# A gated attention with channel mix on one core: all engines in one written order, one scan over four pairs, the second square on ACT, weights in contiguous pieces

## Chip, cores and metric

The kernel runs on one core of one Trainium2 chip. The metric is the device time of one execution in microseconds. The kernel before took 393.07 us, the median of three runs (390.4 to 397.02).

## The reference

Two layers in float32: a linear attention with a decaying state for 4 batches, 8 heads, 768 steps, head size 48, and a channel mix of 384 features with 1024 inner ones.

```python
for t in range(S):
    state = alpha[:, :, t, :, None] * state + einsum('bhd,bhe->bhde', k[:, :, t], v[:, :, t])
    y[:, :, t] = einsum('bhd,bhde->bhe', q[:, :, t], state)
...
xk = mu_k * x + (1 - mu_k) * x_prev        # x: y with the heads side by side
xr = mu_r * x + (1 - mu_r) * x_prev        # x_prev: the row of the step before
k = maximum(xk @ w_k, 0)
v = k * k @ w_v
r = 1 / (1 + exp(-(xr @ w_r)))
out = r * v
```

## The kernel before

**Tiles.** The 24 chunks of 128 steps lie in nine groups, each within one batch: groups 0 to 2 have two chunks (256 columns), groups 3 to 8 have three (384). Heads lie in four pairs, two heads of a pair on partitions 0 to 47 and 64 to 111.

**Attention of a group.** `load` fetches alpha (`al`), k, q and v. `prep_p` makes the running product of alpha, one forward scan per pair (L258), the reciprocal of its last column (L262), and on ACT a check that no alpha is over 1 (`junk`, L265). `prep_gh` multiplies q by the product (L276), scans backward from that reciprocal, again one scan per pair (L281), and multiplies k by it (L284); tables give each product to DVE or POOL, most queries to DVE, most keys of groups of three chunks to POOL. A chunk then needs: `trans`, transposes of k through TensorE (L336) and ACT's copy `ht` (L338); `scores` (L346) and the mask on DVE (`am`, L352); `update` (L399) and `advance`, the state sums on DVE (L411, L415, L417); `intra` and `inter` (L365, L383); `leave` (L425, L431). One `visit` handles `intra`, `inter` and `leave` of a chunk together with `update`, `scores` and `advance` of the next. After the last chunk two DMAs copy borrowed rows inside `xt` (L438), from SP for group 0 and from ACT for the others.

**Channel mix of a group.** `mix` forms xk and xr (i = 0 and 1): for each of three feature tiles a scaling on ACT (L478), a sum on DVE (L479), a rounded high part on ACT (L482) and the difference as low part on DVE (L483). `moe` lists the pieces of TensorE's work: 8 up slices of 9 matmuls (L500), a gate of 9 per chunk (L525), a down of 24 per chunk (L540). Each product of float32 numbers is three products of high and low parts. After an up slice ACT takes the positive part `r` (L508); r squared in float32 comes from ACT in groups 0 and 1 (L510) and from DVE in the others (L512); ACT squares r once more into the rounded high part `kh` (L513), and DVE subtracts to get `kl` (L514). After a down, DVE multiplies by the gate (L545), and SP stores.

**Weights** come as raw words. `split` makes high and low parts of a piece: ACT copies the top half words (L208), DVE shifts and joins (L213), ACT or DVE rounds the high part (L219, L221), POOL or DVE subtracts (L222). There are four pieces of the up, two of the gate and four of the down weights.

**Order.** TensorE and SP follow the written order; ACT, DVE and POOL are ordered by the planner of the framework. `merge` lays the attention of group g+1, with weights, among the pieces of the channel mix of group g; then comes `mix` of g+1. From group 1 on, the load and the whole of `prep` for group g+2 stand at the start of that attention. For group 0 a table `FILL` says at which step weight pieces and the preparations of groups 1 and 2 are put in.

Of the kernel before, what the change touches and what calls it, by code (L numbers as in the profile page):

```python
# [42 lines left out]
LEAD = 12.0  # L43
LEAD0 = 8.0
PAD = 3.0
ENG = {
    "wk": ("AP", "AD", "AP", "AP"),
    "wr": ("DP", "DP"),
    "wv": ("DP", "DP", "AD", "DP"),
}  # L50
K2 = "AAD"
QH = ("DDDD", "PDPD", "PPPP")
QG = ("PDDD", "DPDP", "DDDP")
FILL = [
# [3 lines left out]
]  # L58
FIRST_LOADS = ["k", "wk0", "al", "wk1", "q", "wk2", "wk3", "v"]
WARM = 22  # L60
HOLD = 14
NX = HB - D
# [4 lines left out]


def merge(main, side, lead):
    total = max(sum(w for w, _ in main) - lead, 1.0)  # L70
    load = sum(w for w, _ in side)
    done = spent = 0.0
    side = list(side)
    for w, f in main:
        f()
        done += w
        while side and spent / load <= done / total:
            ws, fs = side.pop(0)
            fs()
            spent += ws  # L80
    for _, fs in side:
        fs()
# [3 lines left out]
def gated_attention_channel_mix(  # L86
# [17 lines left out]
    PE, ACT, DVE, POOL = nc.tensor, nc.scalar, nc.vector, nc.gpsimd  # L104

# [8 lines left out]
    zero = cp.tile([R, R], F32, name="zero")  # L114
    POOL.memset(zero, 0.0)

    hot = pm.tile([R, R], F32, tag="pm", name="hot")
    with tc.manual_schedule(engines={mybir.EngineType.PE}):
        for i in range(WARM):
            PE.matmul(hot, zero, zero, start=True, stop=True)  # L120

    none, *rings = (cp.tile([R, NP * D + HB - D], F32, name=f"st{i}") for i in range(5))
    for t in (none, *rings):
        POOL.memset(t, 0.0)
    tiny = cp.tile([128, 1], F32, name="tiny")
    POOL.memset(tiny, FLOOR)
    mone = cp.tile([128, 1], F32, name="mone")
    POOL.memset(mone, -1.0)
    ones = cp.tile([128, 1], F32, name="ones")
    POOL.memset(ones, 1.0)  # L130
    ACT.activation(ones, ones, AF.Sigmoid)
    POOL.memset(ones, 1.0)
    racc = cp.tile([128, 2 * NG], F32, name="racc")
# [3 lines left out]
    mu = cp.tile([128, 2, NT], F32, name="mu")  # L137

    loaded = {}

    def span(g):
# [678 lines left out]
```

## Time and profile before

| | |
|---|---|
| median of three runs | 393.07 us |
| the profiled execution | 391.8 us |
| its span, first to last instruction | 390.1 us |
| TensorE matmul busy | 332.0 us (85%) |
| DVE busy | 281.6 us (72%) |
| ACT busy | 188.7 us (48%) |
| POOL busy | 65.3 us (17%) |
| mean granted TensorE clock | 0.923 |
| DMA | 35.56 MB, mean 91 GB/s |

An instruction is named by its line, engine, operation and tiles (out<-in). A row of groups gives the count, busy time, mean duration in ns, and the idle time of that engine just before, with what ended it. A row of the timeline gives start and length in us. Ends of matmuls are modelled, and matmuls overlap. POOL's spans are rough.

### The profile page before, as it was taken

How to read it: one execution, taken by the hardware profiler on the slowest of the kernel's cores; microseconds unless marked ns; L12 is line 12 of the kernel's file. 1: busy time of each engine (PE TensorE's matmuls, PEld its weight loads, DVE VectorE, ACT ScalarE, POOL GpSimd, SP SyncE). 2: the span in 40 equal slices, each digit the busy share in tenths (PEclk: the TensorE clock that was granted, in tenths of full speed). 3: DMA queues.
4: the chain of work that ended last, by engine and by line, in shares of the span. 5: the costliest groups of instructions: out<-in, count | busy, mean ns of one | idle time of the engine just before them, and what ended most of it. 6: DMA issues, size and time to landing. Idle time of an engine off the chain costs nothing.

```text
span 390.1 us, 10751 instructions
## 1 busy us (share of the span) xinstructions
PE 332.0 (85%) x4590; PEld 315.5 (81%) x4590; DVE 281.6 (72%) x513; ACT 188.7 (48%) x393; POOL 65.3 (17%) x84
## 2 busy tenths in 40 slices
PE   7542787709995997899979997999999999999993
PEld 6432687709984996799969997999999999999993
DVE  5787989998389639988596959678965476456510
ACT  3356693236563345544355525562754555455500
POOL 5143544550021003203010220003000000000000
PEclk9655769968999799999999998999999999999998
DMA  8978455830703070305510341025100110011001
GB/s 212 273 249 293 136 152 143 233 91 24 212 25 92 12 214 22 91 3 172 142 42 2 100 144 42 3 74 169 44 2 2 37 43 3 3 37 40 0 23 47
DMA packets 15958, 35.56 MB, mean 91 GB/s; under 512 B 1600, under 2 KB 9568, under 8 KB 15904
## 3 DMA queue, kind: packets, MB, share of 16 engines
q1 hardware_dynamic: 14736, 33.72, 29.2%
q10 hardware_dynamic: 1168, 1.09, 1.1%
q8 instruction: 38, 0.62, 0.7%
q14 instruction: 16, 0.13, 0.1%
HBM read 28.90 MB, written 4.72 MB: 86 GB/s over the span
## 4 chain that ended last, share of the span: by engine, by line
PE 47%; DVE 20%; DMA 6%; issue 4%; ACT 3%; ACTq 0%; DVEq 0%
PE pk L500 19%; PE pv L540 13%; PE pg L525 5%; DVE al L281 4%; DMA xt<-xt 4%; DVE pp L258 4%; DVE x L479 3%; PE yu L365 2%; DMA q<-q_p 2%; DVE xkl L483 2%; DVE q L276 1%; PE pt L336 1%; DVE kl L514 1%; PE sp L346 1%; PE yu L399 1%
## 5 line engine op out<-in xcount | busy, mean ns | idle before, releaser
L500 PE MATMUL pk<-xkh,wkh 128*128 128x384 f32 (+1 forms) x216 | 51.4, 345 | 21.7 <-ACT xkh L482 21.7
L540 PE MATMUL pv<-wvh,kl 128*128 128x384 f32 x192 | 64.9, 338 | 2.4 <-DVE kl L514 2.4
L540 PE MATMUL pv<-wvl,kh 128*128 128x384 f32 x192 | 64.7, 337 | 0.0
L540 PE MATMUL pv<-wvh,kh 128*128 128x384 f32 x192 | 64.4, 335 | 0.0
L500 PEld LDWEIGHTS pk<-xkh,wkh 128*128 128x128 f32 x216 | 37.9, 203 | 24.5 <-ACT xkh L482 23.6
L508 ACT ACTIVATE r<-pk 128x384 f32<-128x384 f32 (+1 forms) x72 | 32.3, 454 | 41.2 <-PE pk L500 38.4
L500 PE MATMUL pk<-xkh,wkl 128*128 128x384 f32 (+1 forms) x216 | 49.6, 340 | 0.0
L500 PE MATMUL pk<-xkl,wkh 128*128 128x384 f32 (+1 forms) x216 | 48.6, 335 | 0.1
L284 POOL TENSOR_TENSOR k<-k,al 112x768 f32<-112x768 f32 (+1 forms) x18 | 31.1, 1733 | 91.3 <-DVE al L281 50.0
L512 DVE TENSOR_TENSOR k<-r 128x384 f32<-128x384 f32 (+1 forms) x56 | 30.0, 535 | 22.7 <-ACT r L508 22.1
L478 ACT ACTIVATE x<-xt,mu 128x384 f32<-128x384 f32 (+1 forms) x54 | 28.5, 575 | 35.6 <-DMA xt<-xt 25.5
L514 DVE TENSOR_TENSOR kl<-k,kh 128x384 fp32r<-128x384 f32 (+1 forms) x72 | 36.7, 509 | 11.0 <-ACT kh L513 5.8
L281 DVE TENSOR_TENSOR_SCAN al<-al 112x383 f32<-112x383 f32 (+1 forms) x36 | 39.7, 1137 | 1.3 <-ACT junk L265 1.1
L500 PEld LDWEIGHTS pk<-xkl,wkh 128*128 128x128 f32 x216 | 38.4, 203 | 0.8 <-DVE xkl L483 0.3
L540 PEld LDWEIGHTS pv<-wvh,kl 128*128 128x128 f32 x192 | 36.1, 188 | 3.4 <-DVE kl L514 3.4
L500 PEld LDWEIGHTS pk<-xkh,wkl 128*128 128x128 f32 x216 | 37.2, 202 | 0.9
L258 DVE TENSOR_TENSOR_SCAN pp<-al,tiny 112x384 f32<-112x384 f32 (+1 forms) x36 | 33.9, 963 | 4.2 <-DMA al<-al_p 4.2
L540 PEld LDWEIGHTS pv<-wvl,kh 128*128 128x128 f32 x192 | 36.0, 188 | 0.0
L540 PEld LDWEIGHTS pv<-wvh,kh 128*128 128x128 f32 x192 | 36.0, 188 | 0.0
L513 ACT ACTIVATE kh<-r 128x384 fp32r<-128x384 f32 (+1 forms) x72 | 34.7, 488 | 1.4
L479 DVE SCALAR_TENSOR_TENSOR x<-xt,nu,x 128x384 f32<-128x384 f32 (+1 forms) x54 | 31.9, 631 | 2.7 <-ACT x L478 2.7
L425 ACT COPY xt<-yu 112x512 f32<-112x512 f32 x24 | 14.1, 588 | 35.8 <-DVE st L415 25.3
(149 smaller groups left out, 531.3 us busy)
## 6 DMA issues: line engine op xcount, KB each, us to landing
out<-sig SPq DMA_DIRECT2D x24, 192.0 KB, 1.9
al<-al_p SPq DMA_DIRECT2D x6, 672.0 KB, 5.3
k<-k_p SPq DMA_DIRECT2D x6, 672.0 KB, 4.7
q<-q_p SPq DMA_DIRECT2D x6, 672.0 KB, 7.4
v<-v_p SPq DMA_DIRECT2D x6, 600.0 KB, 4.2
wkraw<-wk_p SPq DMA_DIRECT2D x4, 768.0 KB, 14.6
vraw<-wv_p SPq DMA_DIRECT2D x4, 768.0 KB, 5.5
v<-v_p SPq DMA_DIRECT2D x3, 400.0 KB, 6.6
```

Source lines behind the costliest of these rows:

```text
L258: DVE.tensor_tensor_scan(pp[:, p], al[:, p, :n], tiny[:R].to_broadcast([R, n]), initial=START, op0=ALU.mult, op1=ALU.max,)
L281: DVE.tensor_tensor_scan(back, back, back, initial=al[:, i, n : n + 1], op0=ALU.mult, op1=ALU.bypass)
L284: (DVE if QH[min(g, 2)][p] == "D" else POOL).tensor_tensor(k[:, hp], k[:, hp], al[:, hp, 1:], op=ALU.mult)
L478: ACT.activation(x, xt[:, t, 1 : 1 + n], AF.Copy, scale=mu[:, i, t : t + 1])
L479: DVE.scalar_tensor_tensor(x, xt[:, t, 0:n], nu[:, i, t : t + 1], x, op0=ALU.mult, op1=ALU.add)
L500: PE.matmul(pk, w[:, t, cols], x[:, t], start=part == 0 and t == 0, stop=part == 2 and t == NT - 1,)
L508: ACT.activation(r, pk, AF.Relu)
L512: DVE.tensor_tensor(k2, r, r, op=ALU.mult)
L513: ACT.activation(kh[:, f], r, AF.Square)
L514: DVE.tensor_tensor(kl[:, f], k2, kh[:, f].bitcast(F32), op=ALU.subtract)
L525: PE.matmul(pg, x[:, i, cols], w[:, i], start=part == 0 and i == 0, stop=part == 2 and i == NT - 1,)
L540: PE.matmul(pv, x[:, f, cols], w[:, f], start=f == 0 and i == 0, stop=f == NF - 1 and i == 2,)
```

## The change

All five engines now follow one written order. `prep_p` and `prep_gh` become `fwd`, `bwd`, `qm` and `km`: one forward and one backward scan per group run over all four pairs at once. Each pair gets one more column, in which alpha is 0, and the second operand `fl` of the scans holds a start value in that column (2^30 forward, the reciprocal of the product's last column backward), so that the scan starts anew; elsewhere `fl` holds the floor 2^-50. All q products go to POOL, one chunk and then the rest; of the k products chunk 0 goes to DVE, the rest to POOL.

```diff
-        for p in range(p0, p0 + m):
-            DVE.tensor_tensor_scan(
-                pp[:, p], al[:, p, :n], tiny[:R].to_broadcast([R, n]), initial=START,
-                op0=ALU.mult, op1=ALU.max,
-            )
...
+    def fwd(g):
...
+        DVE.tensor_tensor_scan(
+            flat(pp), flat(al), fl[:, : NP * (n + 1)], initial=START, op0=ALU.mult, op1=ALU.max
+        )
+        junk = p1.tile([R, NP, n + 1], U8, tag="r", name="junk")
+        ACT.activation(junk, al, AF.Relu, bias=mone[:R], accum_out=racc[:R, g : g + 1])
+        DVE.reciprocal(breaks(n), pp[:, :, n - 1])
...
+    def bwd(g):
+        n = span(g)[3]
+        back = flat(loaded["al", g])[:, ::-1]
+        DVE.tensor_tensor_scan(
+            back, back, fl[:, : NP * (n + 1)][:, ::-1], initial=0.0, op0=ALU.mult, op1=ALU.max
+        )
+        if g + 1 < NG:
+            if span(g + 1)[3] != n:
+                POOL.memset(breaks(n), FLOOR)
+            POOL.memset(breaks(span(g + 1)[3]), START)
```

`mix` is called once for each half, with one buffer `x` for three tiles, and makes the three low parts in one instruction. After an up slice ACT squares once in float32; the rounded high part is a copy, on DVE in groups 0 and 1 and on ACT in the others. It comes a little later in the order.

```diff
-            r = p2.tile([128, n], F32, tag="r", name="r")
-            k2 = p1.tile([128, n], F32, tag="k2", name="k2")
+            r = p1.tile([128, n], F32, tag="r", name="r")
             ACT.activation(r, pk, AF.Relu)
-            if K2[min(g, 2) if type(g) is int else 2] == "A":
-                ACT.activation(k2, r, AF.Square)
-            else:
-                DVE.tensor_tensor(k2, r, r, op=ALU.mult)
-            ACT.activation(kh[:, f], r, AF.Square)
-            DVE.tensor_tensor(kl[:, f], k2, kh[:, f].bitcast(F32), op=ALU.subtract)
+            sq = p2.tile([128, n], F32, tag="sq", name="sq")
+            ACT.activation(sq, r, AF.Square)
+            later(0.6, lambda: low(f, sq))
...
+        x = p1.tile([128, NT, n], F32, tag="x", name="x")
         for t in range(NT):
-                x = p2.tile([128, n], F32, tag="x", name="x")
+            ACT.activation(x[:, t], xt[:, t, 1 : 1 + n], AF.Copy, scale=mu[:, i, t : t + 1])
...
+        for t in range(NT):
+            ACT.activation(hi[:, t], x[:, t], AF.Copy)
+        DVE.tensor_tensor(lo, x, hi.bitcast(F32), op=ALU.subtract)
```

In group 0 the downs of both chunks go slice by slice (`across`). The host lays each weight piece out so that a partition reads it in one run; loads are whole tensors; the loads of group 0, of the up weights, of group 1 and of the gate weights are issued in this order, then the down weights. The raw up weights lie in the buffers of the later down weights. The borrowed rows of group 0 are copied from ACT's queue as well. The warm-up of TensorE grows from 22 to 30 products.

The order is a list of marks: a mark is put in before the first piece of TensorE's channel mix whose place (sum of the weights of the pieces before it, near microseconds) is not smaller. `trans` of a chunk is now 0.4 before the first visit and 1.6 before the others.

```diff
+SIDE = {
+    1: (0.2, 5.6, 9.2, 12.2, 15.4),
+    2: (0.2, 5.2, 8.2, 11.2, 13.6, 16.4),
+    3: (0.2, 5.6, 8.8, 12.4, 15.8, 18.4),
+}
+KH = "DDAAAAAAA"
...
+            if g == 0:
+                marks += [
+                    (1.2, lambda: fwd(1)),
+                    (2.5, lambda: qm(1, 0, 1, "P")),
+                    (4.0, lambda: bwd(1)),
...
+                    (6.3, lambda: (begin(1), mix_group(0, 1))),
+                    (7.4, lambda: (trans((1, 0)), visit(None, (1, 0)))),
+                    (7.5, lambda: (conv("r", 0, "A"), conv("r", 1, "A"))),
...
+                    (8.2, lambda: visit((1, 0), (1, 1))),
+                    (8.25, lambda: conv("v", 0, "A")),
+                    (8.3, lambda: (load_al(2), visit((1, 1), None))),
+                    (8.5, lambda: conv("v", 1, "A")),
...
+                    (10.5, lambda: conv("v", 2, "A")),
+                    (11.5, lambda: conv("v", 3, "A")),
+                    (12.5, lambda: (mix_in(1, span(1)[3]), mix_group(1, 0))),
+                    (14.5, lambda: mix_group(1, 1)),
+                    (17.0, lambda: fwd(2)),
...
+                def start_h(h=h, m=m):
+                    bwd(h)
+                    km(h, 0, 1, "D")
+                    km(h, 1, m - 1, "P")
...
+                def after(h=h):
+                    if h + 1 < NG:
+                        fwd(h + 1)
+                        qm(h + 1, 0, 1, "P")
+                        qm(h + 1, 1, GROUPS[h + 1][2] - 1, "P")
+
+                marks.append((at[0], start_h))
+                marks.append((at[0] + 0.1, loads))
+                marks.append((at[1] - 0.4, lambda u=units[0]: trans(u)))
+                marks.append((at[1], lambda u=units[0]: visit(None, u)))
...
+                t0 = at[2 + m]
+                marks.append((t0, mixes))
+                marks.append((t0 + 2.0, lambda h=h: mix_group(h, 1)))
+                marks.append((t0 + 4.5, after))
```

Before these marks, group 0 is prepared as a whole, its attention runs with the first two pieces of the up weights among it, then its first mixed half and the other two pieces (`conv`: `split_top`, `split_or`, `split_hi`, `split_lo`). Group 1 as main group takes row 1 of `SIDE`, group 2 takes row 2, the others take row 3.

More of the change, by code (lines that the diff above doesn't have):

```diff
@@ L42 @@
 DW = D // DQ
[L43 to L49, printed above, removed]
-}
[L51 to L54, printed above, removed]
[3 rows of a table removed]
[L58 to L62, printed above, removed]
+WP = 2 * DM
+WARM = 30
+NX = HB - D
+UP, GATE = 0.16, 0.52
+SIDE = {
+    1: (0.2, 5.6, 9.2, 12.2, 15.4),
+    2: (0.2, 5.2, 8.2, 11.2, 13.6, 16.4),
+    3: (0.2, 5.6, 8.8, 12.4, 15.8, 18.4),
+}
+KH = "DDAAAAAAA"
 def head(i, o):
     return 2 * (2 * (i >> 1) + o) + (i & 1)
[L69 to L82, printed above, removed]
 @with_exitstack
@@ L112, in gated_attention_channel_mix @@
     dp = ctx.enter_context(tc.tile_pool(name="dp", bufs=1, space=DRAM))
[L114 to L120, printed above, removed]
     none, *rings = (cp.tile([R, NP * D + HB - D], F32, name=f"st{i}") for i in range(5))
[L123 to L126, printed above, removed]
+    fl = cp.tile([R, NP * (GMAX + 1)], F32, name="fl")
     mone = cp.tile([128, 1], F32, name="mone")
-    POOL.memset(mone, -1.0)
     ones = cp.tile([128, 1], F32, name="ones")
[L130 to L133, printed above, removed]
+    racc = cp.tile([128, NG], F32, name="racc")
     pbeg = cp.tile([128, NG * NP], F32, name="pbeg")
@@ L192, in gated_attention_channel_mix, with load_al @@
[L192 to L206 removed]
+    def load_al(g):
+        b, c0, nck, n = span(g)
+        t = p2.tile([R, NP, n + 1], F32, tag="al", name=f"al{g}")
+        loaded["al", g] = t
+        at = NP * (b * S + c0 * C + g)
+        nc.sync.dma_start(
+            t.rearrange("r p t -> r (p t)"), al_p[:, at : at + NP * (n + 1)]
+        )
@@ new lines, in flush, with spend, run @@
+    def flush(all_=False):
+        while True:
+            ready = [d for d in due if all_ or d[0] <= clock[0] + 1e-9]
+            if not ready:
+                return
+            d = min(ready)
+            due.remove(d)
+            d[2]()
+    def spend(w):
+        clock[0] += w
+        flush()
+    def run(pieces, marks):
+        marks = sorted(marks, key=lambda m: m[0])
+        t = 0.0
+        for w, f in pieces:
+            while marks and marks[0][0] <= t + 1e-9:
+                marks.pop(0)[1]()
+            f()
+            t += w
+            spend(w)
+        for _, f in marks:
+            f()
@@ new lines, in scores @@
+    def scores(u, sp):
+        g, c = u
+        h, q = loaded["k", g], loaded["q", g]
+        for p in range(NP):
+            for s, j in sides:
+                rr = slice(j * HB, j * HB + D)
+                t0 = c * C + s * HC
+                PE.matmul(
+                    sp[s * HC : (s + 1) * HC, j, p * HC : (p + 1) * HC],
+                    h[rr, p, t0 : t0 + HC], q[rr, p, t0 : t0 + HC],
+                    start=True, stop=True,
+                )
+        am[u] = p2.tile([C, 2, NP, HC], F32, tag="am", name=f"am{g}_{c}")
+        DVE.tensor_tensor(
+            am[u], sp[:, :, : NP * HC].rearrange("c j (p t) -> c j p t", p=NP),
+            mask.unsqueeze(1).unsqueeze(1).to_broadcast([C, 2, NP, HC]), op=ALU.mult,
+        )
```

751 lines of the change are left out of this document (376 added, 375 removed), and 3 rows, old and new, of the table FILL.

## The prediction

> **What bounds the kernel now.** I read the work of each engine in ten windows first, cut where a group's first up matmul starts. Columns: length, busy microseconds of PE, weight loads, DVE, ACT and POOL with counts, granted clock, DMA.
>
> ```profile
> 0.00:35.00 35.00, 17.04 (x308) 15.09 (x308) 24.82 (x42) 14.27 (x22) 15.30 (x36) 0.68 0.86 247
> 35.00:84.70 49.70, 32.40 (x402) 30.19 (x402) 47.99 (x73) 26.34 (x62) 24.24 (x20) 0.81 0.55 163
> 84.70:114.90 30.20, 27.84 (x386) 26.49 (x387) 20.73 (x45) 19.30 (x51) 1.34 (x4) 0.90 0.33 99
> 114.90:154.40 39.50, 32.35 (x536) 30.20 (x536) 29.79 (x58) 16.86 (x40) 7.05 (x7) 0.91 0.32 89
> 154.40:195.20 40.80, 38.43 (x552) 36.43 (x551) 34.12 (x59) 19.95 (x41) 7.19 (x6) 1.00 0.35 98
> 195.20:236.20 41.00, 38.40 (x570) 36.64 (x569) 32.35 (x60) 20.79 (x43) 5.43 (x6) 1.00 0.24 68
> 236.20:278.00 41.80, 39.60 (x553) 37.91 (x552) 34.22 (x65) 22.02 (x45) 4.54 (x5) 0.96 0.23 72
> 278.00:315.80 37.80, 37.80 (x568) 36.41 (x567) 24.43 (x51) 20.43 (x40) 0.19 (x1) 1.00 0.06 21
> 315.80:353.80 38.00, 38.00 (x554) 36.61 (x553) 21.96 (x46) 19.10 (x37) 0.00 (x0) 1.00 0.07 22
> 353.80:390.10 36.30, 30.10 (x174) 29.49 (x172) 11.23 (x22) 9.62 (x19) 0.00 (x0) 0.97 0.07 24
> ```
>
> Groups 6 and 7 are PE alone: 37.9 us each, PE never idle. Group 8 has no attention beside it: 30.1 us of PE, so a chunk of attention costs PE (37.9-30.1)/3 = 2.6. Before 84.7 the limit is DVE, busy 48.0 of 49.7 us in group 0. Then the waits of PE, and its timeline, which show where those windows are cut:
>
> ```profile
> PE pk L500 <- ACT xkh L482: 21.7, 6, 9.3
> PE pt L336 <- DVE k L284: 6.7, 5, 2.6
> PE yu L365 <- DVE am L352: 4.6, 3, 2.4
> ...
> 22.20 0.92 PE L346 MATMUL sp<-q,k 48*64 48x64 f32 x23 [1.47 <-issue]
> 25.03 1.14 PE L365 MATMUL yu<-am,v 64*64 64x64 f32 x32 [1.91 <-DVE am L352]
> 35.02 0.98 PE L500 MATMUL pk<-xkh,wkh 128*128 128x256 f32 x2 [8.00 <-ACT xkh L482]
> ...
> 84.70 0.97 PE L500 MATMUL pk<-xkh,wkh 128*128 128x256 f32 x2 [9.28 <-ACT xkh L482]
> 87.88 0.58 PE L500 MATMUL pk<-xkh,wkh 128*128 128x256 f32 x1 [2.20 <-ACT xkh L482]
> ...
> 353.77 0.68 PE L500 MATMUL pk<-xkh,wkh 128*128 128x384 f32 x3
> 354.29 0.68 PE L500 MATMUL pk<-xkh,wkl 128*128 128x384 f32 x3
> ```
>
> Here is to be seen that PE waits for two things: for the first mixed half of a group (xkh: 8.0, 9.3 and 2.2 us, the work that DVE was late with), and for keys and masked scores. At full clock three matmuls of 384 columns take 0.52 us, nine (one up slice) 1.56.
>
> **Working of the change.** The sum is made against this execution: span 390.1, its time 391.8, so 1.7 us lie around the span; it is 1.3 under the median of 393.07.
>
> *Until the first up matmul (35.0 now).*
>
> ```profile
> 4.19 1.27 DVE L258 TENSOR_TENSOR_SCAN pp<-al,tiny 112x256 f32<-112x256 f32 x2 [4.19 <-DMA al<-al_p]
> 12.50 0.42 DVE L284 TENSOR_TENSOR k<-k,al 112x256 f32<-112x256 f32 x1
> 17.65 4.09 DVE L258 TENSOR_TENSOR_SCAN pp<-al,tiny 112x256 f32<-112x256 f32 x4
> ```
>
> The keys of group 0 are ready at 12.9. With whole loads alpha lands later (twice the bytes of the first piece, an estimate of 5.1), then two scans of 2.4 each, a reciprocal 0.2, 0.8 lost to POOL and a key product 0.7 (prices below) give 11.6: minus 1.3. The scan of group 1 (4.09) no longer stands in front of the masks, so the waits of 1.5 and 1.9 go: minus 3.4. The last hop of 8.0 becomes 5.2 from the last visit to the landed rows less its own 1.0, 2.5 for the half and 0.8 for queueing, 7.5: minus 0.5. Sum 29.8; bounds 27 (every wait gone) and 35. Weights in pieces three times as long cost nothing: the windows show 247 GB/s before 35.0 and no PE wait on a weight load; their cover is the DVE chain. The last-column zeros of al_p and the longer warm-up lie in the first 12 us.
>
> *Group 0 (49.7 now).* What DVE has to do before the first mixed half of group 1 is there, at these prices:
>
> ```profile
> L213 DVE SCALAR_TENSOR_TENSOR rraw<-rraw,tops 128x768 uint32<-128x768 uint32 x1 | 1.0, 962 | 0.5 <-ACT tops L208 0.5
> L514 DVE TENSOR_TENSOR kl<-k,kh 128x256 fp32r<-128x256 f32 x24 | 10.0, 416 | 5.4 <-ACT kh L513 3.8 <-ACT k L510 1.2
> L352 DVE TENSOR_TENSOR am<-sp,mask 128x512 f32<-128x512 f32 x15 | 10.2, 683 | 1.6 <-PE sp L346 1.6
> L222 POOL TENSOR_TENSOR wvl<-vraw,wvh 128x768 fp32r<-128x768 f32 x3 | 6.1, 2039 | 8.7 <-DVE wvh L221 8.7
> L276 POOL TENSOR_TENSOR q<-q,pp 112x256 f32<-112x256 f32 x4 | 4.4, 1117 | 4.5 <-PE sp L383 3.8 <-DMA q<-q_p 0.6
> L258 DVE TENSOR_TENSOR_SCAN pp<-al,tiny x36: 659/943/2326, 4.2 to 241.4; 112x384 f32<-112x384 f32 x24, 112x256 f32<-112x256 f32 x12
> L281 DVE TENSOR_TENSOR_SCAN al<-al x36: 717/1005/2237, 5.8 to 264.3; 112x383 f32<-112x383 f32 x24, 112x255 f32<-112x255 f32 x12
> ```
>
> A scan of 256 columns takes 0.66, one of 384 takes 0.94: 2.2 ns a column and 0.1 fixed. So one scan over four pairs is 2.4 us for 1028 columns, 3.5 (backward 3.6) for 1540: it saves three fixed parts, some 0.3, and holds DVE in one piece. Restart columns: no row; their bounds are 0 and the four columns' 9 ns. DVE list: shift-or of seven pieces at 0.96 and a half one, 7.3; two casts, 1.1; eight casts of kh moved from ACT, no row of that form, between 0.1 and 0.42, taken 0.3: 2.4; eight kl at 0.42, 3.3; two scans 4.8; a key product 0.7; two mixed halves (three sums at 0.42 and one merged difference at 0.96 each), 4.4; two masks at 0.68 and nine state and output sums of 128 to 192 columns, each under the 0.42 of 256 and taken at 0.31, 4.2. Together 28.2. POOL meanwhile: seven low parts of 2.04, one of 1.0, three products of 512 columns at 1.6 (between 1.12 and 2.04): 20.1. POOL and DVE hinder each other:
>
> ```profile
> 178.43 1.01 DVE L281 TENSOR_TENSOR_SCAN al<-al 112x383 f32<-112x383 f32 x1 [0.35 <-ACT junk L265]
> 179.81 4.07 DVE L281 TENSOR_TENSOR_SCAN al<-al 112x383 f32<-112x383 f32 x3
> 180.96 2.11 POOL L284 TENSOR_TENSOR k<-k,al 112x768 f32<-112x768 f32 x1 [13.60 <-DVE al L281]
> ```
>
> Three scans take 4.07 instead of 3.03 while a POOL product of 2.11 runs: 0.5 us of DVE for each of POOL, so 10.0. With 2.3 for ACT, which stands between its two halves of each weight piece until DVE has done the shift-or, group 0 takes 40.5; bounds 32 (28.2 and a third of the rest) and 50 (as now). The Trainium skill, SBUF — State Buffer, section Who interferes with whom, says more: a DVE instruction with two SBUF inputs and a reading GpSimd one exclude each other, and the later waits the whole length. By that page alone the 10.0 would be 20.1, and the sum 394; the row shows half of it. It speaks against this change, which hands POOL all query products and two thirds of the keys.
>
> *The chain from group to group.* Now the products for a group are ready a group ahead. In the written order forward scan and backward scan of the next group stand behind both mixed halves of this one:
>
> ```profile
> 339.04 0.69 PE L365 MATMUL yu<-am,v 64*64 64x64 f32 x32
> 340.97 1.22 ACTq L438 DMA_DIRECT2D xt<-xt  x2
> 344.21 1.12 ACT L478 ACTIVATE x<-xt,mu 128x384 f32<-128x384 f32 x2 [1.43 <-DMA xt<-xt]
> L513 ACT ACTIVATE kh<-r 128x384 fp32r<-128x384 f32 x48 | 25.2, 526 | 1.1
> ```
>
> From the last visit to the landed rows 5.2 us; each half 4.5 (three scalings at 0.56, the last sum at 0.6, the last rounding 0.53, then one difference of 1152 columns, 1.4; the second half waits for it, x having one buffer), 9.0; an output product 0.5; forward scan 3.5, reciprocal 0.2, backward scan 3.6, key product 0.7. Sum 22.7 until the next group's transposition can start. PE's list prices its pieces in microseconds (nine up matmuls 1.56, three others 0.52): 29.6 for a group of 384 columns, 19.7 for one of 256. The last visit stands at 15.8, the next group's transposition at 5.2, so PE is there after 13.8, 1.1 for the visit and 5.2: 20.1. So PE stands 2.6 there: groups 4 to 7 take 37.9+2.6 = 40.5, together 162.0. Group 2 has 256 columns and its last visit at 13.6: 6.1+1.1 are left, the first mixed half comes at 8.3, so 1.1 of wait, and the chain ends 9.2 behind PE in group 3: 47.1. In group 1 the halves cost 3.4 (256 columns), the chain 20.5, PE is there after 7.5+1.1+4.8 = 13.4 (last visit at 12.2): 7.1 in group 2, whose own work is 28.5 (group 1's 27.0 from 87.9 to 114.9, less about 1.1 of cold start, plus a chunk of 2.6): 36.7. In group 1 the second half, both scans and the key stand 9.4 behind the first one, PE is there after 5.2: 4.2, with 25.9 of its own 30.1. Group 8 keeps 36.3.
>
> The queues that are passed: SP's loads go out ahead of the outputs but into buffers that came free a group earlier; the two DMAs of borrowed rows move to ACT for group 0 (0.6 each there, under the flight between the last two dated rows). The third ACT instruction per up slice makes three of at most 0.53, 1.6 us against 1.56 of PE, and its cover is the 2.6 us of attention per chunk; without it 0.04 a slice. The square that leaves DVE from group 2 on (one pass a slice) frees DVE in windows where PE does not wait for it, so by itself nothing.
>
> **Sum.** 29.8+40.5+30.1+36.7+47.1+162.0+36.3 = 382.5, with 1.7 outside 384.2, called 384. The beginning gives 14; the chain gives 7 of it back.
>
> **Rivals.** *Covered chain:* if halves and scans overlap more than the order says, or PE has other work ahead of the transposition, the four terms 4.2, 8.2, 9.2 and 10.4 go: 352; half of them 368. For it: groups 6 and 7 show PE can run at 37.9. Against: one x buffer and DVE in written order. *Slower by the shared way of POOL and DVE:* the query products (1.6 and about 2.5) start with the forward scan's end, just as the backward scan and the key product do. If POOL goes first each time, 4.1 us more per group, in groups 1 to 7: 28.7, giving 413; it is slower by 2% once it costs 2.4 a group. For it: the 4.07 row; against: that row shows half the length. The Trainium skill's page SBUF — State Buffer stands on this rival's side. *No gain in the beginning:* ACT waits inside each weight piece and group 1 starts at 84.7 as now: 14.4 more, 398. *It doesn't do what it says:* the order now is already near the written one and nothing moves: 392.
>
> **How the numbers follow.** Forecast 0.44 (its own range 372 to 397: 0.25 faster, 0.17 same, 0.02 slower), covered 0.24 (0.23 faster), POOL 0.12 (0.10 slower, 0.02 same), beginning 0.12 (0.01, 0.09, 0.02), nothing 0.08 (0.01, 0.06, 0.01). Faster 0.50, same 0.35, slower 0.15, where 2% is about what a measurement of this kernel can tell from no change. Range 356 to 404: the half-covered chain below, all but the full POOL price above; outside it some 0.09 and 0.11.
>
> **What would show it.** First up matmul near 30 and group 1's near 70; then PE waiting, in front of the first transposition of each group, for the key product of chunk 0, longest in group 3 (about 9 us), 2 to 3 us in groups 4 to 7, none in group 8; forward scans of 3.5 and backward ones of 3.6 us. Wrong if groups 3 to 7 take 38 us each, if a scan takes over 5, or if group 1 starts after 80.

## The result, and the profile after

The changed kernel takes 447.03 us (median of 4 runs, 446.22 to 448.51), the kernel before 391.74 beside it: a ratio of 1.143, 95% interval 1.137 to 1.149. The forecast was 384. Ratios here compare undisturbed runs, and one run of a later kernel, with 415.89 us at a granted clock of 0.804, is left out of its figures. The profiled execution took 448.51 with a span of 446.7. Its windows, cut at each group's first up matmul, with the columns of the prediction's first fence:

```profile
0.00:35.98 35.98, 17.58 (x324) 16.14 (x325) 17.46 (x28) 9.44 (x16) 14.36 (x24) 0.66 0.86 289
35.98:91.62 55.64, 37.09 (x403) 34.06 (x403) 36.88 (x51) 28.03 (x52) 19.97 (x16) 0.70 0.17 50
91.62:125.57 33.95, 29.10 (x387) 27.64 (x387) 22.19 (x41) 15.15 (x37) 6.79 (x8) 0.90 0.35 101
125.57:165.68 40.11, 31.05 (x535) 29.14 (x534) 24.73 (x37) 18.75 (x45) 10.62 (x8) 0.87 0.28 82
165.68:218.99 53.31, 42.22 (x551) 39.15 (x552) 32.55 (x43) 28.76 (x57) 10.62 (x7) 0.90 0.20 58
218.99:265.94 46.95, 41.73 (x569) 39.50 (x568) 27.91 (x40) 23.65 (x47) 10.84 (x8) 0.93 0.27 75
265.94:313.61 47.67, 41.98 (x553) 39.52 (x552) 26.93 (x38) 23.64 (x47) 10.63 (x7) 0.93 0.25 73
313.61:361.05 47.44, 41.74 (x567) 39.57 (x568) 28.13 (x40) 23.64 (x47) 10.83 (x8) 0.93 0.25 74
361.05:406.95 45.90, 41.29 (x553) 39.01 (x553) 27.16 (x38) 22.08 (x45) 10.63 (x6) 0.93 0.06 18
406.95:446.70 39.75, 31.85 (x174) 31.20 (x173) 7.57 (x20) 13.53 (x27) 0.00 (x0) 0.93 0.09 32
```

| stretch | before | forecast | after |
|---|---|---|---|
| to the first up matmul | 35.0 | 29.8 | 36.0 |
| group 0 | 49.7 | 40.5 | 55.6 |
| group 1 | 30.2 | 30.1 | 34.0 |
| group 2 | 39.4 | 36.7 | 40.1 |
| group 3 | 41.0 | 47.1 | 53.3 |
| groups 4 to 7 | 158.5 | 162.0 | 188.0 |
| group 8 | 36.3 | 36.3 | 39.8 |

In groups 4 to 7 the matmuls are the same, yet PE is busy 41.3 to 42.0 us instead of 38 to 40, at a clock of 0.93: part of the loss is waiting, part is slow matmuls. DVE is busy 27 to 28 us of 46 to 48 there, so it is not short of time, and the suspicion falls on its order. Some waits of the whole span (total, times, longest):

```profile
ACT sq L501 <- DVE kl L482: 43.5, 10, 7.9
...
PE pt L314 <- DVE k L246: 32.7, 7, 7.5
...
PE yu L385 <- ACT ht L316: 13.4, 12, 4.4
...
PE pk L492 <- ACT r L499: 8.3, 6, 3.1
```

The first row is ACT, whose next square needs a buffer that DVE's low part frees, and that low part stands behind the scans in DVE's order. The wait for the key product (L246, 32.7 us) was 6.7 us in 5 times before; it is the chain that the prediction described. Here is its end in group 5, from the timelines of DVE, POOL and PE (start, length):

```profile
265.51 3.36 DVE L211 TENSOR_TENSOR_SCAN pp<-al,fl 112x1540 f32<-112x1540 f32 x1
269.92 3.51 DVE L230 TENSOR_TENSOR_SCAN al<-al,fl 112x1540 f32<-112x1540 f32 x1
273.46 2.48 DVE L246 TENSOR_TENSOR k<-k,al 112x512 f32<-112x512 f32 x1
...
269.01 6.39 POOL L241 TENSOR_TENSOR q<-q,pp 112x512 f32<-112x512 f32 x2 [35.93 <-DVE pp L211]
...
276.00 0.60 PE L314 MATMUL pt<-ident,k 112*128 112x112 f32 x4 [3.23 <-DVE k L246]
278.06 1.10 PE L385 MATMUL yu<-v,ht 64*64 64x48 f32 x32 [0.83 <-ACT ht L316]
...
281.17 1.16 PE L492 MATMUL pk<-xkh,wkl 128*128 128x384 f32 x3
```

Between the rows of one engine others are left out; the next group's transposition is the row of L314. The scans cost what the forecast said (3.36 and 3.51). The key product takes 2.48 instead of 0.7: it ends 0.54 us after POOL's second query product, which is through at 275.4. PE stands 3.23 us, and then three matmuls take 1.16 us instead of 0.68. The windows of these microseconds show why (the number behind the five engines is the granted clock):

```profile
272.70:276.00 3.30, 0.07 (x1) 0.00 (x1) 3.27 (x3) 0.00 (x0) 3.30 (x3) 1.00 1.00 285
278.00:280.00 2.00, 1.94 (x35) 1.85 (x36) 2.00 (x3) 0.00 (x1) 1.64 (x4) 0.50 0.98 265
282.00:284.00 2.00, 2.00 (x10) 1.90 (x9) 0.56 (x1) 0.58 (x2) 0.00 (x0) 0.50 0.00 0
284.70:287.00 2.30, 2.30 (x122) 2.04 (x124) 0.56 (x1) 0.97 (x2) 0.00 (x0) 1.00 0.00 0
```

After a stand of 3.2 us the clock is at half for some 6.5 us. Theory A, made from this: each group loses a stand and then the clock behind it, both because the next group's scans stand behind the mixed halves in the written order. Rivals: the written order is too rigid in many places (B); POOL shuts DVE out (C); the parts themselves are dear, in whatever order (B2).

### The profile page after: what moved, and what is told of

Its sections match the earlier page's. It is cut to its first block, busy times and chain, and to the rows that moved or that the text cites. A ratio compares the mean times of both kernels' runs of the same rounds, so it can differ in the third digit from the quotient of the medians.

```text
span 446.7 us, 10634 instructions
## 1 busy us (share of the span) xinstructions
PE 355.6 (80%) x4606; PEld 334.9 (75%) x4606; DVE 251.5 (56%) x368; ACT 206.7 (46%) x417; POOL 105.3 (24%) x92
## 4 chain that ended last, share of the span: by engine, by line
PE 38%; DVE 29%; ACT 20%; DMA 6%; issue 4%; ACTq 1%; POOL 1%; SPq 0%; DVEq 0%; POOLq 0%
PE pk L492 8%; PE pg L512 7%; PE pv L527 7%; DVE al L230 6%; DVE pp L211 5%; ACT x L463 5%; DMA xt<-xt 5%; PE yu L385 4%; DVE k L246 4%; PE yu L347 3%; PE sp L326 3%; ACT sq L501 3%; PE pt L314 2%; ACT xkh L468 2%; DVE xkl L469 2%
## 5 line engine op out<-in xcount | busy, mean ns | idle before, releaser
L241 POOL TENSOR_TENSOR q<-q,pp 112x512 f32<-112x512 f32 (+1 forms) x18 | 49.2, 2753 | 217.5 <-DVE pp L211 102.7
L482 DVE TENSOR_TENSOR kl<-sq,kh 128x384 fp32r<-128x384 f32 (+1 forms) x72 | 47.6, 668 | 51.2 <-ACT kh L479 50.7
L492 PEld LDWEIGHTS pk<-xkh,wkh 128*128 128x128 f32 x216 | 41.0, 216 | 28.4 <-ACT xkh L468 12.5
L501 ACT ACTIVATE sq<-r 128x384 f32<-128x384 f32 (+1 forms) x72 | 35.2, 489 | 45.5 <-DVE kl L482 43.5
L492 PE MATMUL pk<-xkl,wkh 128*128 128x384 f32 (+1 forms) x216 | 54.6, 367 | 0.4 <-DVE xkl L469 0.4
L499 ACT ACTIVATE r<-pk 128x384 f32<-128x384 f32 (+1 forms) x72 | 32.6, 452 | 41.5 <-PE pk L492 41.2
L464 DVE SCALAR_TENSOR_TENSOR x<-xt,nu,x 128x384 f32<-128x384 f32 (+1 forms) x54 | 29.1, 593 | 33.7 <-ACT x L463 33.7
L314 PE MATMUL pt<-ident,k 112*128 112x112 f32 x96 | 17.6, 319 | 35.2 <-DVE k L246 32.7
L492 PEld LDWEIGHTS pk<-xkl,wkh 128*128 128x128 f32 x216 | 40.8, 221 | 1.7 <-DVE xkl L469 0.7
L314 PEld LDWEIGHTS pt<-ident,k 112*128 112x128 f32 x96 | 13.4, 173 | 38.2 <-DVE k L246 34.8
L463 ACT ACTIVATE x<-xt,mu 128x384 f32<-128x384 f32 (+1 forms) x54 | 27.4, 570 | 31.0 <-DMA xt<-xt 16.9
L492 PEld LDWEIGHTS pk<-xkh,wkl 128*128 128x128 f32 x216 | 40.6, 213 | 0.2
L527 PEld LDWEIGHTS pv<-wvh,kh 128*128 128x128 f32 x192 | 36.9, 192 | 3.6 <-ACT sig L518 3.4
L415 ACT COPY xt<-yu 112x512 f32<-112x512 f32 x24 | 14.1, 589 | 54.2 <-DVE st L403 35.6
L527 PEld LDWEIGHTS pv<-wvl,kh 128*128 128x128 f32 x192 | 36.9, 192 | 1.6 <-POOL wvl L194 1.6
L527 PEld LDWEIGHTS pv<-wvh,kl 128*128 128x128 f32 x192 | 36.9, 192 | 0.0
L332 DVE TENSOR_TENSOR am<-sp,mask 128x512 f32<-128x512 f32 x24 | 16.5, 688 | 27.4 <-PE sp L326 25.2
## 6 DMA issues: line engine op xcount, KB each, us to landing
v<-v_p SPq DMA_DIRECT2D x6, 600.0 KB, 10.4
```

Source lines behind the costliest of these rows:

```text
L241: (DVE if eng == "D" else POOL).tensor_tensor(q, q, loaded["pp", g][:, :, ts], op=ALU.mult)
L314: PE.transpose(pt[:, p, :], h[:, p, c * C : (c + 1) * C], ident[:R, :R])
L463: ACT.activation(x[:, t], xt[:, t, 1 : 1 + n], AF.Copy, scale=mu[:, i, t : t + 1])
L464: DVE.scalar_tensor_tensor(x[:, t], xt[:, t, 0:n], nu[:, i, t : t + 1], x[:, t], op0=ALU.mult, op1=ALU.add)
L482: DVE.tensor_tensor(kl[:, f], sq, kh[:, f].bitcast(F32), op=ALU.subtract)
L492: PE.matmul(pk, w[:, t, cols], x[:, t], start=part == 0 and t == 0, stop=part == 2 and t == NT - 1,)
```

## The experiments

One run and one profile each where no interval is given; the kernel before took 389.0 to 391.5 in the same sessions.

**The place of the forward scan.** First the scan, its check on ACT and the query products were moved into the middle of the attention:

```diff
-                marks.append((t0 + 4.5, after))
+                marks.append((at[2] + 1.2, after))
```

> Only the mark of the next group's forward scan, its check on ACT and its query products moves: from 4.5 behind the last visit's mark plus halves to 1.2 behind the first visit that ends a chunk, so that at a group's start only the backward scan (3.5 us) and one key product (0.7 us alone) stand ahead of the first transposition. Theory A (the chain through both halves and both scans makes PE stand 3.3 us in groups 4 to 7, 7.3 in 2 and 3, and each stand is followed by some 7 us at half clock, 3.4 us more): the waits of the transposition for the key product go to under 1 us, groups 4 to 7 take 39.5 to 41 us instead of 45.8 to 47.7, total 395 to 410. Rival B (the written order of ACT and DVE itself is too rigid, with many small waits: low parts behind scans, the second square behind low parts): the stand goes, but the groups stay over 44, total over 430. Rival C (POOL and DVE exclude each other, wherever the query products lie): the 4 us of lock move with the products into the middle of the group, groups take 43 to 44.

Measured 424.1: 23 us less, not 37 or more. Groups 4 to 7 took 41.8, 44.0, 43.9, 39.2; two of them lie where rival C put all four. The stand ahead of the transposition went, and the key product of these groups took 0.69 us again, as the query products had moved along with the scan. But a new stand came in the middle (timelines of ACT and PE, group 5 of this run):

```profile
272.74 1.56 ACT L215 ACTIVATE junk<-al,mone 112x1540 uint8<-112x1540 f32 x1
275.38 0.51 ACT L316 COPY ht<-pt 128x448 f32<-128x448 f32 x1
...
275.95 0.60 PE L385 MATMUL yu<-v,ht 64*64 64x48 f32 x15 [2.42 <-ACT ht L316]
```

ACT's check of alpha had moved along and now stood ahead of the copy `ht`. So it was left where the change had it, split from the scan:

```diff
+                marks.append((at[2] + 1.2, after))
+                if h + 1 < NG:
+                    marks.append((t0 + 4.5, lambda h=h: over(h + 1)))
```

> As the first experiment (forward scan and query products of the next group in the middle of the attention), but ACT's check of alpha (1.75 us) is split from the scan and stays where the change had it, behind the mixed halves. In the first experiment groups 4 to 7 took 41.8, 44.0, 43.9, 39.2, and in the three that had a check ACT's copy ht came 2.4 us late, after which the clock fell in two of them. Theory A2 (one instruction of ACT in the wrong place of the written order is the rest of it): 39 to 40.5 in each of main groups 4 to 7, total 410 to 418. Rival (the lock between POOL's key product and DVE's low part, 1.1 us, delays the masks just as much): groups stay at 42 to 44 and the total at 420 to 424.

Measured 415.6, the groups 40.9, 41.3, 40.9, 39.2, at full clock:

```profile
251.50:292.75 41.25, 38.86 (x553) 36.97 (x552) 25.74 (x37) 23.38 (x47) 8.09 (x7) 1.00 0.30 85
```

The total is in the range of theory A2, the groups 4 to 6 a little above it. Two marks are worth 31 of the 55 us. Theory A holds for the steady groups, with one reservation: the move took POOL's lock of 1.8 us out of the chain together with the scan, and no run separates the two. Group 3 still took 47.0 and group 0 55.9.

**The clock by itself.** Products of zeros ran while PE waited:

```diff
+        for i in range(heat):
+            PE.matmul(pt[:R, 0, :], zero, zero, start=True, stop=True)
...
-                marks.append((at[1] - 0.4, lambda u=units[0]: trans(u)))
+                marks.append((at[1] - 0.4, lambda u=units[0]: trans(u, 56 if u[0] in (3, 4) else 24)))
```

> Nothing moves; ahead of the first transposition of each group from 3 on PE gets products of zeros into the transposition's own PSUM tile, 56 for groups 3 and 4 and 24 for the others, which run while it waits for the key product. This prices the clock apart from the stand. Theory A: the stands stay (3.3 us in groups 4 to 7, filled), but the half clock after them goes: 3.4 us less in each of the main groups 4 to 7, some 5 in 2 and 3, total 425 to 430. Rival (the low clock is set by something else, such as the whole mean load, or the half speed after the stand is waiting and not clock): 444 or more.

Measured 444.4, the rival's number. But the clock is 1.00 in groups 2 to 7, so the stands did set it, and the profile shows why so little is gained: the filler was too long. From the timelines of PE and DVE of this run, group 5, and then its window:

```profile
274.74 4.88 PE L314 MATMUL pt<-st 112*112 112x112 f32 x48
279.46 0.55 PE L316 MATMUL pt<-ident,k 112*128 112x112 f32 x4
...
275.61 2.49 DVE L246 TENSOR_TENSOR k<-k,al 112x512 f32<-112x512 f32 x1
```
```profile
268.09:312.83 44.74, 43.37 (x600) 41.62 (x600) 27.19 (x38) 23.60 (x47) 10.66 (x7) 1.00 0.28 78
```

The key was ready at 278.1 and the filler held PE until 279.46, so 1.4 of the 44.74 is its own. Against 47.67 the clock costs 2.9 + 1.4 = 4.3 us in this group. The same working gives 3.5, 4.0 and 2.5 in groups 4, 6 and 7, and 2.3 and 2.5 in groups 2 and 3. With it group 5 adds up: 37.9 of matmuls, 3.23 of stand, 0.64 + 0.83 + 0.73 of smaller waits for ACT, 4.3 of clock, together 47.6.

**The written order as a whole.** ACT, DVE and POOL back in the planner's hands:

```diff
-    with tc.manual_schedule(engines={ET.PE, ET.SP, ET.Activation, ET.DVE, ET.Pool}):
+    with tc.manual_schedule(engines={ET.PE, ET.SP}):
```

> Only TensorE and SyncE keep the written order; ACT, DVE and POOL are ordered by the framework's planner, as in the kernel before. All other parts of the change stay. Theory A (the loss comes from where the scans and the keys stand in the written order): the planner may take the scans ahead of the halves, groups 3 to 7 then take under 42 and the total 395 to 415. Rival B2 (the loss comes from the parts themselves: one long scan, all query products on POOL, the square on ACT, one x): within 2 per cent of 447. Also open: the planner may order worse than the written order in group 0.

Measured 410.8: of the 55 us lost, the order of these three engines is 36. The other 19 are what the parts cost in the planner's order; that is not yet a price of the parts, since the planner may place them badly too (the last run below shows where).

**The beginning.** The loads of the gate weights and of three down pieces went to ACT's queue, behind the conversion of the up weights:

```diff
-        fetch("r", wr_p, 0, WP, lambda s, d, n: p1.tile(s, d, tag="wst0", name=n))
...
         split_lo("k", 3, "P")
+        fetch("r", wr_p, 0, WP, lambda s, d, n: p1.tile(s, d, tag="wst0", name=n), nc.scalar)
...
```

> The changed kernel, with the loads of the gate weights and of three pieces of the down weights issued from ACT's queue behind the four up pieces' conversion, in place of SP's queue at 11 to 25 us. Theory F (the first mixed half waits 7.2 us for the borrowed rows, because their two DMAs queue behind 10.4 MB of loads at 290 GB/s, which end at 34): the rows land by 30, the first up matmul moves from 36.0 to 31 to 32. Rival (the rows take 7 us whatever is ahead of them): it stays at 35.5 to 36. What group 0 does with weights that come later is open: total 440 to 450.

Measured 445.3, first up matmul at 31.2. The first scaling of the first half in the timeline of the kernel after, then in that of this run with the first up matmul, then the window of this run in which the rows are there and no load moves (last number, GB/s):

```profile
34.32 1.31 ACT L463 ACTIVATE x<-xt,mu 128x256 f32<-128x256 f32 x3 [5.31 <-DMA xt<-xt]
```
```profile
27.41 1.30 ACT L463 ACTIVATE x<-xt,mu 128x256 f32<-128x256 f32 x3
...
31.21 0.58 PE L492 MATMUL pk<-xkh,wkh 128*128 128x256 f32 x1 [7.74 <-ACT xkh L468]
```
```profile
27.00:30.00 3.00, 0.00 (x0) 0.00 (x0) 2.40 (x2) 1.71 (x4) 1.52 (x1) 0.50 0.00 0
```

The two row copies, 48 KB each, were issued until 27.1 in the kernel after and landed at 34.3, when the other loads ended (289 GB/s over the window up to 35.98: 10.4 MB); with those out of the way they were issued until 25.7 and had landed by 27.4. Then group 0 took 57.5, so that 3.0 of the 4.8 us were left where group 1 starts (88.7 against 91.6). Next, the high parts of gate and down weights from ACT to DVE:

```diff
-                    (7.5, lambda: (conv("r", 0, "A"), conv("r", 1, "A"))),
+                    (7.5, lambda: (conv("r", 0, "D"), conv("r", 1, "D"))),
...
-                    (8.25, lambda: conv("v", 0, "A")),
+                    (8.25, lambda: conv("v", 0, "D")),
...
```

> Only the rounded high parts of the gate and down weights go from ACT to DVE (six casts of about 0.95 us). Concerns group 0, which took 58.1 us where 40.5 were forecast. Theory D (ACT in written order stands 8.7 us in group 0 between the two halves of its work on each weight piece, and the copy ht and the sigmoid behind them make PE wait 4.4 and 3.1 us, which also cools the clock): group 0 takes 46 to 52 and the total falls by 6 to 12, to 435 to 441. Rival (group 0 is held by the low part on POOL and by the late loads): under 3 us.

Measured 444.0, group 0 49.4 instead of 55.6: the theory's 6 us. The total fell by only 3.0 us against the median (4.5 against the profiled execution) and missed the theory's 435 to 441; groups 1, 2 and 7 got about 1 us longer each. ACT's two kinds of wait for DVE's shift-or were 5.0 us in 4 pieces and 3.7 in 2 in the kernel after, 8.7 where the forecast had 2.3.

**Parts of the change alone, in the kernel before.** The square on ACT (`K2 = "AAD"` to `"AAA"`):

> The kernel before with one part of the change alone: the float32 square of groups 2 to 8 on ACT in place of DVE (two squares and the positive part on ACT, the difference on DVE), ordered by the planner. The prediction costs it at nothing, its cover being the 2.6 us of attention per chunk. If so: within 1 per cent of the kernel before. Rival: three ACT instructions of 0.5 us per up slice fill PE's 1.56 us, copies of attention come in between, PE waits for r: 1.5 to 3 us more in each of groups 2 to 8, 10 to 20 in all.

Measured 396.4, 6 us more (1.5%, one run each): 42.5 and 42.2 us in groups 3 and 4 against 41.0 and 40.8. All query products on POOL (`QG` to `"PPPP"` for all groups):

> The kernel before with one part of the change alone: all query products on POOL (two pairs, 768 columns of three chunks, about 1.9 us each), planner order kept. Theory C (whole exclusion): DVE loses what POOL takes, the groups with a preparation (2 to 6 as main group 1 to 5) get 1 to 3 us longer, total 395 to 405. Rival (the exclusion hides under PE's work, as there is slack of DVE): 388 to 394.

Measured 402.7, 12 us more. A wait appears that the kernel before does not have, and group 3 grows from 41.0 to 45.1 (the waits and the windows of this run):

```profile
DVE pp L258 <- POOL q L276: 16.9, 3, 6.4
```
```profile
155.23:200.35 45.12, 40.15 (x552) 37.99 (x552) 33.85 (x58) 20.25 (x42) 13.94 (x9) 0.92 0.34 93
```

In sum 12 and 6 are near the 19 that the planner's version leaves, but not in their places: that version lost 9.0 us in group 6 and 4.6 in group 4, these two runs 0.9 and 0.5 in group 6, 2.4 and 1.4 in group 4. The agreement of the sums explains nothing yet.

**The same parts undone in the written order.** From the run with scan early and check late (415.6), first the products on DVE, the key products of groups 2 to 8 and the query products of groups 3 to 8 (those of group 2 stay on POOL):

```diff
-                        qm(h + 1, 0, 1, "P")
-                        qm(h + 1, 1, GROUPS[h + 1][2] - 1, "P")
+                        qm(h + 1, 0, GROUPS[h + 1][2], "D")
...
-                    km(h, 1, m - 1, "P")
+                    km(h, 1, m - 1, "D")
```

> The kernel of the run with scan early and check late (415.6), with all query and key products of groups 2 to 8 on DVE instead of POOL (2.0 and 1.3 us more for DVE per group). Theory C (POOL's product shuts DVE out for its whole length, so handing products to POOL costs DVE as much as it saves): DVE's low part at the group's start takes 0.5 instead of 1.6 us, the groups are the same or 0.5 to 1 us shorter, total 409 to 415. Rival (the shared time is cheap and POOL's products save DVE time that matters): 418 to 425.

Measured 423.2. Groups 4 to 6 stayed (41.2, 41.1, 41.4), groups 1 to 3 got 1.7 to 2.7 longer. So in this form POOL's exclusion costs no more than the work on DVE would, and rival C is not the cause of what is left. Then the square on DVE:

```diff
-            ACT.activation(sq, r, AF.Square)
+                DVE.tensor_tensor(sq, r, r, op=ALU.mult)
```

> The kernel of the run with scan early and check late (415.6), with the second square of groups 2 to 8 back on DVE. In the kernel before the same part alone cost 1.4 us in groups 3 and 4 and 0.4 to 0.5 in 5 and 6. If ACT's written order is what is left (copy ht late by 0.7 us a group, low parts behind ACT): groups 4 to 6 fall from 41 to 39.5 to 40.3, total 408 to 413. Rival (DVE is as tightly ordered, a square behind a scan makes low and high part late): 416 to 425.

Measured 468.4, 53 us more, far outside both expectations. From the timelines of ACT and DVE in group 5 of this run:

```profile
284.62 0.53 ACT L482 ACTIVATE kh<-sq 128x384 fp32r<-128x384 f32 x1 [2.94 <-DVE sq L507]
285.05 0.47 ACT L502 ACTIVATE r<-pk 128x384 f32<-128x384 f32 x1
287.55 0.52 ACT L482 ACTIVATE kh<-sq 128x384 fp32r<-128x384 f32 x1 [2.02 <-DVE sq L507]
...
285.18 1.86 DVE L485 TENSOR_TENSOR kl<-sq,kh 128x384 fp32r<-128x384 f32 x1 [0.59 <-ACT kh L482]
286.96 0.55 DVE L507 TENSOR_TENSOR sq<-r 128x384 f32<-128x384 f32 x1
```

A slice now goes ACT, DVE, ACT, DVE in a fixed order, each standing until the other is done, and ACT's next `r` stands behind `kh`. In the kernel before ACT made `kh` from `r` by itself and did not wait for DVE's square. With `kh` made from the square, a square on DVE makes ACT wait in this order; ACT squaring twice, as before, was not run in a written order.

**Towards a better order.** Backward scan, check and key products of the next group ahead of the mixed halves, the high parts on DVE as above, and the last flags later:

```diff
+                    marks.append((t0 - 0.01, lambda h=h: over(h + 1)))
+                    marks.append((t0 + 0.01, lambda h=h: keys(h + 1)))
...
-                marks.append((8 * 3 * UP * 3, judge))
+                marks.append((8 * 3 * UP * 3 + 4.0, judge))
```

> Everything that the theory names is moved, nothing is taken out: forward scan and query products in the middle of the attention; ACT's check, the backward scan and the key products of the next group right behind the last visit, ahead of both mixed halves, where DVE now waits for the rows; high parts of gate and down weights on DVE as in the run before; the last check of the flags four microseconds later. Theory A: groups 4 to 7 take 38 to 39.5, group 0 49, the last one 37, total 385 to 398, the level of the kernel before. Rival C (POOL's key product of 3.5 us locks the sums of the halves): the first up matmul of the next group waits 2 to 3 us for its mixed half, total 400 to 410.

Measured 434.2; both expectations were too low. The backward scan waited 3.5 us for ACT's check and pushed the halves back, and behind them in DVE's order stood the gate's multiplication, which frees the accumulator of the next up slice (waits of this run):

```profile
PE pk L495 <- DVE sig L535: 17.6, 5, 4.5
```

Against the run with scan early and check late, groups 1 to 7 got 1.2 to 6.1 us longer; group 0 gained by its high parts (49.5), and the last group by the mark of the flags (36.6 instead of 41.0). So the mark of the flags, and the gains of the other runs, were put into one kernel, with the preparation of group 1 around its first mixed half and the visits of groups 1 and 2 0.4 to 2.4 us earlier:

```diff
+        fwd(1)
+        over(1)
         mix_in(0, span(0)[3])
         mix_group(0, 0)
...
+        bwd(1)
+        qm(1, 0, 2, "P")
...
-    1: (0.2, 5.6, 9.2, 12.2, 15.4),
-    2: (0.2, 5.2, 8.2, 11.2, 13.6, 16.4),
+    1: (0.2, 5.6, 8.6, 11.4, 13.6),
+    2: (0.2, 4.8, 7.2, 9.6, 12.0, 14.0),
```

> All places that the runs so far named are moved in one written order, with no work left out: scan early and check late (415.6 by itself); high parts of the gate and down weights on DVE (6.3 us less in group 0 by itself); late loads of those weights (first up matmul at 31.2 instead of 36.0, group 0 then 1.8 longer); the last check of the flags four microseconds later (4.4 less in group 8); the preparation of group 1 ahead of and behind the first mixed half instead of among the up slices, which takes away the wait of 4.8 us of group 0; visits of groups 1 and 2 as main groups some 2 us earlier. If the gains add: 415.6 - 6.3 - 3.0 - 4.4 - 3 to 5 = 397 to 399, and with 2 us from the earlier visits 395. Rival (in group 0 the gains are the same one, since DVE is busy 43 of 49 us there): 403 to 406.

Measured 399.7, near the 397 to 399 of the added gains; the same kernel, timed four times:

> The merged kernel once more, timed in rounds: 397 to 403 expected from its single run of 399.7, so 2 per cent behind the kernel before and some 10 per cent ahead of the change.

401.34 against 391.03, ratio 1.027 (1.021 to 1.033): 46 us better than the change, still slower than the kernel before. Two attempts to mend it. In group 0, the forward scan of group 1 later and the weights' low parts on DVE:

```diff
-            split_lo(key, i, "P")
+            split_lo(key, i, "D")
```

> The merged kernel (399.7) with two changes of its beginning: the forward scan of group 1 stands behind the up weights' conversion instead of ahead of the first mixed half (there it held the half until 35.1, although the rows had landed at 29.2), and the low parts of the gate and down weights are made by DVE (0.96 us) instead of POOL (2.0 to 2.5 us). Theory C (POOL shuts DVE out, so in group 0, where DVE is the limit, POOL's work costs more than DVE's own): first up matmul at 31 to 32, group 0 45 to 48, total 392 to 396. Rival (DVE is the limit by its own list, low parts on POOL help): group 0 over 50, total 398 to 402.

Measured 403.2: the first up matmul came at 33.1 instead of 35.6, and group 0 took 49.6 instead of 47.5, so group 1 starts where it did (82.7 against 83.1). Theory C's 45 to 48 did not come; but the run changes two things in group 0 at once, and which of them cost the 2 us is not shown. Then `KH = "DDDDDDDDD"`, rounding on DVE:

> The merged kernel (399.7) with the rounded high part kh on DVE in all groups (the table's A becomes D), so that ACT does two instructions per up slice instead of three. Theory G (in written order ACT is full while up slices and attention run together: 1.56 us of three instructions against 1.56 of PE, plus copies; hence ht and the copy to xt come late): the waits for ht (0.7 to 1.3 per visit) and xt go, groups 4 to 6 fall from 40.3, 41.1, 41.2 to 38.5 to 39.5, total 388 to 394. Rival (DVE, whose rounding stands behind scans and sums, is late instead, as with the square on DVE): 403 or more.

Measured 410.6, and every group from 1 on longer; the low part came late behind the scans, and ACT waited for its buffer (ACT in group 5):

```profile
255.75 0.52 ACT L504 ACTIVATE sq<-r 128x384 f32<-128x384 f32 x1 [2.05 <-DVE kl L485]
```

> Both of the two kernels before this one together. If both theories hold the gains add: 383 to 390, at or below the kernel before; if only one holds, 392 to 397; if neither, over 400.

408.04, ratio 1.049 (1.038 to 1.060): over 400, as expected if neither theory holds. Last, the merged kernel under the planner:

> The merged kernel (399.7) with ACT, DVE and POOL ordered by the framework's planner, TensorE and SyncE in the written order. With the marks of the change the planner gave 410.8, 36 less than the written order. If the parts (query products on POOL, square on ACT, which cost 12 and 6 us in the kernel before when put in alone) are what is left, it stays at 395 to 402, as the merged written order; if what is left is the written order of the three engines, it falls to 380 to 392.

408.92, ratio 1.043 (1.035 to 1.051). The marks that gained 46 us in the written order change nothing for the planner (410.8 before them), and the merged order is 8 us better than the planner's. Where the planner loses is to be seen in the windows of groups 5 and 6 of this run, and in the timelines of DVE and PE in group 6:

```profile
245.11:286.99 41.88, 38.71 (x552) 36.99 (x552) 25.16 (x38) 24.12 (x47) 6.92 (x7) 1.00 0.30 83
286.99:333.49 46.50, 41.83 (x569) 40.03 (x569) 27.21 (x46) 24.17 (x47) 6.77 (x6) 0.93 0.25 75
```
```profile
309.46 3.37 DVE L233 TENSOR_TENSOR_SCAN al<-al,fl 112x1540 f32<-112x1540 f32 x1 [0.74 <-ACT junk L219]
312.74 0.67 DVE L335 TENSOR_TENSOR am<-sp,mask 128x512 f32<-128x512 f32 x1
...
314.34 0.69 PE L350 MATMUL yu<-am,v 64*64 64x64 f32 x32 [2.27 <-ACT xt L418]
```

The planner puts the backward scan, now one piece of 3.4 us, ahead of the mask and the state sum that PE and ACT wait for. In group 6, and likewise in group 4 (45.5), a wait of 1.25 follows and the clock falls to 0.50; in group 5 the same scan leaves PE a wait of 1.48 and the clock stays. In the run with the planner and the first marks it is the same (45.4, 41.4 and 46.9 in groups 4, 5 and 6). So much of its loss there is the place of the long scan and the clock behind it. What keeps the merged order 10 us behind the kernel before lies in groups 1, 3 and 6 (33.5, 44.6 and 41.1 us in the run of 399.7, against 30.2, 41.0 and 37.9); which part or place causes it is not shown.

## Why the prediction was wrong

*What held.* The chain from group to group: stands of 7.2 and 7.5 in groups 2 and 3 (8.2 and 9.2 forecast), 3.2 to 3.5 in 4 to 7 (2.6); the scans' price. That 2.6 came so near is in part luck. From the last visit in group 4 to the first transposition in group 5 DVE's chain took 24.9 us instead of 22.7, with 1.8 of POOL's lock and 1.0 for two gate multiplications that the sum did not have, and PE was later too, after 21.7 instead of 20.1. The 4.2 of group 1 did not come as a stand for keys: there PE waited 3.12 for `r`, behind the second half and the check in ACT's order, and the key was ready when PE came to it. The forecast's own test of the beginning, a start of group 1 after 80, came out against it (91.6).

*"So PE stands 2.6 there: groups 4 to 7 take 37.9+2.6 = 40.5"* is the step that failed most, 26 us in four groups. The stand was nearly right (2.8 too short in four groups), what follows it was missing: 2.5 to 4.3 us a group of half clock, together 14 (zeros as filler), and some 2 of small waits for ACT, together 8. That is 25 of the 26. The trace of before had the sign: two matmuls of 256 columns took 0.97 us behind a wait of 9.28, where three of 384 take 0.68; it was used once, as 1.1 of cold start in group 1. The same term is missing in groups 2 and 3 (2.3 and 2.5 us, clock 0.87 and 0.90).

*"PE waits for two things"* left out a third: the waits for ACT's copy `ht`, 11.3 us in the kernel before, which the list of waits carries under a separate name for each matmul output. Groups 3 to 5 had one of 1.8 to 2.2 us each, yet the sum takes 37.9 as the work of groups 4 and 5.

*"The third ACT instruction per up slice ... its cover is the 2.6 us of attention per chunk"* and *"by itself nothing"* for the square: 6 us under the planner, where PE's waits for the copy `ht` add up to 14.9 us against 11.3 before. ACT's copies use the same cover, and in the written order they stand behind the third instruction.

*"Weights in pieces three times as long cost nothing ... their cover is the DVE chain."* The loads ran faster (289 GB/s against 247), but the row copies of group 0 queued among them: 11.4 us went from the last visit (22.9) to the landed rows (34.3), where the sum had 5.2. The first up matmul came at 36.0, not 29.8; with those loads later, at 31.2.

*"Group 0 takes 40.5"* was a list of DVE. Its total came out (36.9 us busy against 38.2), but DVE was not the limit: ACT stood 8.7 us between its halves of the weight pieces (2.3 in the sum), PE waited for ACT's copy 4.4 and its sigmoid 3.1, and the clock was 0.70. PE also waited 4.8 for the first key and 2.6 for `r`. The high parts moved to DVE took 6.2 of the 15 us away; the rest of group 0 is not separated by runs.

*"Group 8 keeps 36.3":* the flags' last product moved into the last up slice and waited 2.05 for DVE, at half clock after; 3.4 us, gone with a later mark.

*The rival of POOL and DVE* gave 413 by a lock of 4.1 a group in the chain. The lock is there at its whole length, as the Trainium skill's page SBUF — State Buffer, section Who interferes with whom, has it, and not at the half that the 4.07 row suggested: the key product took 2.48 for 0.7. In the chain that is 1.8 us a group. But taking POOL's products away did not help (423.2 against 415.6), in a form where the scan and the query products had left the chain. What the lock's 1.8 by itself cost in the kernel after, no run shows. In the kernel before the query products on POOL cost 12 us, with a wait of DVE for them.

What stays open: why groups 4 to 6 still take 40.3 to 41.2 us in the merged order at full clock, 2.4 to 3.2 above their matmuls. The visible waits there (`ht` 0.7 to 0.8, and in groups 5 and 6 one of 1.0 to 1.4 that ends with PE's own issue) make up 0.8 in group 4 and some 2 in the others. The kernel before took 40.8 and 41.8 in groups 4 and 5 as well, so against it only group 6 is a loss. Also open is what each part costs by itself: the 12 and 6 us come from single runs in the kernel before, their sum does not fit the planner's version group by group, and neither the long scan nor the weights' layout was run alone.

## What to carry to other kernels

When all engines follow one written order, go through each engine's queue and ask what a late instruction holds up behind it: the scan of the next group belongs where its engine is idle and its result not yet needed, and whatever is tied to it (here a check on another engine) has to be placed by itself. Count a wait of the matmul engine not by its length alone but with the slow matmuls behind it. Try a move of work between engines under the order in which it will run, since the square cost 6 us on ACT under a planner, and in a written order 53 us on DVE, where ACT then had to wait for it.

## What was unexpected of the hardware

- After a stand of 3.23 us the granted clock fell only 2 us after work had begun again (0.91 in 276 to 278) and stayed at 0.50 until about 284.5. The Trainium skill's page TensorE: Matmul & The Clock Gate, section What's actually happening, has half rate after an idle window of about 3.4 us, and full rate after as much steady work. The fall comes near that; the return took some 6.5 us here, with small waits in between, and 3.2 in group 8, where there were none. A wait of 2.05 us in group 8, shorter than the page's window, was enough for matmuls of 1.16 instead of 0.68. Its length alone does not decide: in the kernel before the clock stayed at 1.00 behind a wait of 2.22 us in group 4 (200.8 to 202.8) and was 0.50 behind one of 2.20 in group 5 (241.1 to 243.0).
- POOL and DVE excluded each other in both directions: the two query products took 6.39 us beside the backward scan and the key product, 3.71 in the run with the scan early, where DVE ran neither beside them. The second of them ended 1.97 us after the scan (2.18 is its time in that run), and the key product ended 0.54 after it.
- Two row copies of 48 KB took 7.2 us to land while the loads of another queue kept all DMA engines busy, under 2 us without.
